# Four weight conversions of the second MLP, taken from the first two pairs of blocks into block 1

## The chip, the cores and the metric

The kernel runs on one core of a Trainium2 chip. The metric is the device time of one execution in microseconds; where several executions are timed, their median counts. TensorE is called PE in the profile, VectorE DVE, ScalarE ACT, GpSimd POOL and SyncE SP; POOL and SP issue nearly all of the transfers, each from a queue of its own.

## The reference

Attention in chunks of 64 over 8 x 8 heads of 576 x 64, then an MLP with softplus (512 to 2048 to 512), then a second one that takes the largest of three products (512 to 768) and multiplies it by w_out (768 to 512). There are 4608 tokens.

```python
scores = scale * np.matmul(q_c, k_c.transpose(0, 1, 2, 4, 3))      # chunks of 64
attn = np.exp(scores - max); attn = attn / (sum + 1e-09)
x = np.matmul(attn, v_c)                                           # 4608 x 512
h = x @ w_in
g = np.maximum(h, 0.0) + np.log1p(np.exp(-np.abs(h)))
x = g @ w_out                                                      # 4608 x 512
h = np.maximum(np.maximum(x @ w1, x @ w2), x @ w3)
out = h @ w_out2                                                   # 4608 x 512
```

The inputs come as float64, which the chip reads as pairs of 32-bit words. Each weight has to be turned into float32 by integer and float operations on DVE before it can be used.

## The kernel before

The tokens are nine blocks of 512. Blocks 0 to 2 go through the first MLP in steps (`mlp1`): step (b, j) is one h product of block b with the j-th of sixteen slices of w_in (L805, into `ph`), softplus on ACT, a cut into a high and a low part `g` on ACT and DVE (the L288 rows `g<-tmp,g`), and one o product (L825, into `acc`). Each product takes about 2.7 us of PE. The steps of the first two blocks are taken in turns: (0,0-3), (1,0-7), (0,4-15), (1,8-15), and then block 2. Blocks 3 to 8 go in three pairs; a pair's first product is made in eight units with seven products in place of eight (`UnitA`, L1120, into `ph` and `one`), its second one by `mlp1_out` (L1419, into `acc`), and in the last pair in another seven-product form (L1342). Beside this the attention of the later tokens runs in tiles: loads of q and k (L443) and v (L468), transposes on DVE (L698, L699), products into `aps` (L503), a softmax (ACT L562; DVE L554, L558, L590, L591), a transposed p (L751) that is stored to `pd` (L755) and read back turned (L760, `s<-pd`) by SP, and the next product. In the pairs the attention products go to `one` and the like (L597).

The units need differences of weight slices. `weightsa` makes them in blocks 1 and 2 on DVE and ACT from the slices that are still in SBUF, and POOL stores them to `wac` and `wae` (L1027); the units read them back on POOL's queue (L1045). The two halves of a pair also store parts to DRAM, such as `gd` and `wso` (L1233), and partial sums of the first two blocks go through `partd` (L782 reads them back into `tmp` buffers).

The second MLP comes last, and its weights are converted ahead of time by `early(n, due, after)`. There are 24 conversions: numbers 0 to 17 are slices of w1, w2 and w3, numbers 18 to 23 of the last w_out. A conversion of the first kind is
- a load of 512 KB from the input by POOL (L318, into an `s` slot),
- seven operations on DVE: L332, L339, L346, L351, L357, L360 and an add at L288 (`tmp<-tmp,tmp`), in two `tmp` buffers,
- a store of 256 KB to `w2d` by SP (L869).

All of it, with every other piece of work, is an operation of a planner. Each has a due time in an idealised clock (a step counts 5.44 us), the operations that it needs, and the buffers that it takes from pools. `Plan.order` then simulates the engines and starts, on each engine that comes free, the ready operation with the earliest due time; the order in which they start is the order of the program. Each engine, and each queue, then runs its own list in that order, so an instruction that waits holds up all that stands behind it on its engine. A conversion's load may not start before the product given in `after`; the last operation is due `EARLY` = 8 steps after the place from which it was asked. The table `EARLIES` says how many conversions each unit of each pair asks for. No more than two conversions are in the works at a time (a buffer called "early").

Of the kernel before, what the change touches and what calls it, by code (L numbers as in the profile page):

```python
# [183 lines left out]
def tile_kernel(ctx: ExitStack, tc: tile.TileContext, q, k, v, w_in, w_out, w1, w2, w3, wo2, out):  # L184
# [790 lines left out]
    EARLY = 8  # L975
    GATE = 7
    SPLITS = 6
    EARLIES = ((0, 0, 1, 1, 1, 1, 1, 1), (1,) * 8, (2, 2, 1, 1, 1, 1, 1, 1))
    GROUPS = (0, 1, 2, 3, 4, 6, 7)
    LATE_GROUPS = (1,)  # L980
    SPLIT = 1
# [716 lines left out]

    def strassen():

        outs, earlies = [], 0
        tile_at = HP * NP + 2 * HP + 2

        def out(n=1):
            last = None
            for out_of, *which in outs[:n]:
                last = out_of(*which)
            del outs[:n]
            return last

        def group():
            nonlocal tile_at
            if tile_at <= NTILE + 1:
                attention(tile_at, [first_loads[11]], True)
            tile_at += 1

        splita(0)
        pairs = (NB - NP) // 2
        for q in range(pairs):
            A, B = NP + 2 * q, NP + 2 * q + 1  # L1720
            old = None
            sevens = Sevens(q) if q in SEVENS else None

            def later(m, f):
                outs.append((sevens.along, m, f) if sevens else (mlp1_out, A, 2 * m + f))

            for n, m in enumerate(ORDER[q]):
                clock[0] = T0 + STEP * NJ * A + 17.7 * n
                new = UnitA(q, m)
                begin = new.p1()  # L1730
                mark["unit", q, n] = begin
                if ("unit", q, n) in COMBOS:
                    combos(COMBOS.index(("unit", q, n)), [begin], clock[0] + 30.0)
                if n == SEVENS_LOAD and sevens:
                    mark["sevens", q] = begin
                for _ in range(EARLIES[q][n]):
                    early(earlies, clock[0] + STEP * EARLY, [begin])
                    earlies += 1
                if q == pairs - 1:
                    mark[n] = begin  # L1740
                if not sevens:
                    out()
                if old:
                    old.p5()
                    old.p4()
                    if sevens:
                        out()
                    later(old.n, 1)
                new.p6()
                if old:  # L1750
                    old.p3()
                else:
                    out()
                new.p2()
                if not old:
                    out()
                new.p7()
                if n in GROUPS:
                    group()
                out()  # L1760
                later(m, 0)
                old = new
            clock[0] = T0 + STEP * NJ * A + 17.7 * (NJ // 2)
            mark["load", q] = begin
            mark["late", q] = old.p4()
            later(m, 1)
            out()
            old.p5()
            out()
            old.p3()  # L1770
            if sevens:
                outs.extend((sevens.step, p, n2) for p in (5, 4, 3, 6, 7) for n2 in range(NJ // 4))
                while len(outs) > (4 if q == pairs - 1 else 0):
                    out()
                continue
            todo = [(mlp1_out, B, 2 * m + f) for m in ORDER[q] for f in range(2)]
            outs.extend((*todo[i], (h,)) for h in range(2) for i in range(2))
            outs.extend(todo[2:])
            for j in range(NJ - 2):
                o = out()  # L1780
                if ("out", q, j) in COMBOS:
                    combos(COMBOS.index(("out", q, j)), [o], clock[0] + 30.0)
                if j in LATE_GROUPS:
                    group()
                if j == SPLIT and q + 1 < pairs:
                    splita(q + 1)
        mark[5] = mark[6]
        clock[0] = T1
        for late, at in enumerate((mark[FIRST], mark["step", *MORE[2]])):
            weights3(late, [at])  # L1790
        both = [Buf("ph"), Buf("ph"), Buf("aps", fresh=four_banks)]
        accs = [Buf("acc") for _ in range(2)]
        banks = [Bank(both[:1], lambda: both[2].t[0]), Bank(both[1:], lambda: both[2].t[1])]
        banks += [Bank([z], lambda z=z: z.t) for z in accs]
        D = range(NJ2 // 2)
        gate = [mark["step", *MORE[1]]]
        for q in range(NB // 3):
            u = Triple(q, banks, gate)
            u.g = {}
            todo = [(s, d) for d in D for s in (0, 1)] + [(s, d) for s in range(2, 12) for d in D]  # L1800
            todo += [(s, d) for d in D for s in (12, 13)] + [(14, d) for d in D]
            if q == 0:
                todo[:6] = [(0, 0), None, None, (1, 0), None, None, (0, 1), (2, 0), (0, 2), (1, 1), (1, 2)]
                todo = [p for n, p in enumerate(todo) if p != (2, 0) or n < 11]
            for p in todo:
                if p is None:
                    out()
                    continue
                begin = u.product(*p, alloc=both if both[0].first is None else [])
                if p == (11, 0):  # L1810
                    u.late = begin
                if p == (14, 2):
                    gate = [begin]
            for c in range(3):
                for d in D if (q, c) != (NB // 3 - 1, 2) else D[:-1]:
                    u.out(c, d)
            banks = [u.main[1], u.main[2], u.spare, u.main[0]]
        for h in range(2):
            u.out(2, D[-1], range(2 * h, 2 * h + 2))
# [17 lines left out]
    for j in range(NJ):  # L1837
# [4 lines left out]
        for t in range(HP, 2 * HP) if j == 1 else ():  # L1842
            attention_first(t, [line["load"]])
    tiles = 2 * HP
    for n, (b, j, first, last) in enumerate(steps):
        if n >= NJ and n % (NJ // HP) == 0:
            t = HP + n // (NJ // HP)
            t = 2 * HP + (n - NJ) // 2
            while tiles <= t + 1 and tiles < 22:
                attention(tiles, [first_loads[tiles if tiles < 2 * HP + 3 else NJ - 1]])  # L1850
                tiles += 1
        h = mlp1(b, j, first, last)
        if ("step", b, j) in COMBOS:
            combos(COMBOS.index(("step", b, j)), [h], T0 + STEP * (n + 4))
        if b == NP - 1 and j % 2 == 0:
            weightsa(j // 2, [before_last], lead)
        if (b, j) == (1, NJ // 2):
            lead = h
        before_last = h if j % 2 == 0 else before_last
# [38 lines left out]
```

## Time and profile before

| | us |
|---|---|
| median of three timed runs | 1371.14 |
| the three runs | 1365.4, 1371.14, 1371.9 |
| the profiled execution | 1365.48 |
| its span, first to last instruction | 1363.6 |
| busy: PE / DVE / ACT / POOL | 1333.2 / 983.7 / 545.0 / 321.7 |
| DMA moved | 289.38 MB, 212 GB/s in the mean |

The share of a busy engine is an average over stages. Blocks 0 to 2 fill the trace up to about 330 us, the pairs follow until about 840 us, and the second MLP is the rest. What a shift of work is worth is read from the stretch that it leaves and the stretch that it enters: which wait of PE ends there, what it waited for, and how long before their use the results of the other engines are ready. The granted PE clock is full in all of the stretches that are spoken of here (0.994 in the mean of the span, with the only drop near the start).

### The profile page before, as it was taken

What the parts mean: (1) busy time and instruction counts of PE and PEld (TensorE: products, weight loads), DVE (VectorE), ACT (ScalarE), POOL (GpSimd) and SP (SyncE); (2) the same over time, 40 slices, a digit from 0 to 9 for tenths busy, and PEclk for the clock granted to TensorE, in tenths of its full rate; (3) what the DMA queues carried; (4) which work ended last, traced back from release to release, by engine and by line L of the source; (5) the groups of instructions that cost most, each with busy time, mean ns of one, the idle gap of its engine ahead of it and who ended that gap; (6) DMA issues with size and microseconds to landing.
All of it is one profiled execution on the core that took longest, in us unless ns stands there. A gap on an engine that the chain in (4) does not pass through costs nothing.

```text
span 1363.6 us, 23089 instructions
## 1 busy us (share of the span) xinstructions
PE 1333.2 (98%) x8616; PEld 1094.0 (80%) x8616; DVE 983.7 (72%) x1527; ACT 545.0 (40%) x1199; POOL 321.7 (24%) x561
## 2 busy tenths in 40 slices
PE   5899999999999999999999999999999999999998
PEld 4788887888888887787788887888888888888887
DVE  8999965797576898657868898779714597145951
ACT  4544434464544645445535454432123222132211
POOL 2011555542233324323211122121111122011100
PEclk8999999999999999999999999999999999999999
DMA  8565567677689999978966789655644465344401
GB/s 254 159 201 154 134 181 201 189 273 228 169 257 258 267 302 301 280 252 297 366 209 237 259 311 338 234 192 193 219 162 144 155 231 206 141 148 154 139 25 68
DMA packets 218863, 289.38 MB, mean 212 GB/s; under 512 B 121601, under 2 KB 146625, under 8 KB 218753
## 3 DMA queue, kind: packets, MB, share of 16 engines
q0 software_dynamic: 53792, 178.26, 38.1%
q1 hardware_dynamic: 164144, 108.87, 26.9%
q8 instruction: 68, 1.11, 0.3%
q10 hardware_dynamic: 816, 0.79, 0.2%
q14 instruction: 43, 0.34, 0.1%
HBM read 196.61 MB, written 91.23 MB: 211 GB/s over the span
## 4 chain that ended last, share of the span: by engine, by line
PE 86%; DVE 5%; issue 4%; DMA 2%; POOL 1%; ACT 1%; SPq 0%; DVEq 0%; POOLq 0%; ACTq 0%
PE acc L1567 14%; PE both L1567 13%; PE acc L825 10%; PE ph L805 9%; PE ph L1120 8%; PE acc L1419 7%; PE one L1120 6%; PE both L1665 6%; PE acc L1665 5%; PE acc L1342 2%; PE ph L1342 2%; PE acc L1265 2%; DVE s L288 1%; PE aps L503 1%; POOL rv L468 1%
## 5 line engine op out<-in xcount | busy, mean ns | idle before, releaser
L288 DVE TENSOR_TENSOR s<-s,s 128x1024 f32<-128x1024 f32 (+3 forms) x222 | 213.8, 992 | 11.8 <-DMA x2d<-s 5.5
L1419 PE MATMUL acc<-g,s 128*128 128x512 f32 x768 | 184.5, 393 | 3.0 <-ACT tmp L281 2.2
L1419 PEld LDWEIGHTS acc<-g,s 128*128 128x128 f32 x768 | 142.6, 188 | 35.2 <-ACT tmp L281 3.1
L1120 PE MATMUL ph<-s,s 128*128 128x512 f32 x576 | 144.1, 389 | 1.4 <-DMA s<-wac 0.7
L805 PE MATMUL ph<-s,s 128*128 128x512 f32 x576 | 140.4, 394 | 0.0
L825 PE MATMUL acc<-g,s 128*128 128x512 f32 x576 | 139.8, 392 | 0.0
L1120 PEld LDWEIGHTS ph<-s,s 128*128 128x128 f32 x576 | 108.0, 188 | 24.6 <-DMA s<-wac 1.2
L805 PEld LDWEIGHTS ph<-s,s 128*128 128x128 f32 x576 | 108.3, 189 | 23.1
L825 PEld LDWEIGHTS acc<-g,s 128*128 128x128 f32 x576 | 107.3, 188 | 22.6
L281 ACT CAST s<-s 128x512 fp32r<-128x512 f32 (+1 forms) x106 | 86.3, 831 | 93.4 <-DVE s L1598 31.2
L1567 PE MATMUL acc<-s,s 128*128 128x512 f32 x452 | 120.3, 389 | 0.0
L1550 POOL DMA_DIRECT2D s<-w2c x105 | 56.0, 533 | 266.2 <-PE both L1567 87.5
L281 ACT CAST g<-s 128x1024 fp32r<-128x1024 f32 (+1 forms) x64 | 58.7, 919 | 144.6 <-PE both L1567 37.3
L1567 PE MATMUL acc<-g,s 128*128 128x512 f32 x400 | 110.0, 389 | 0.0
L1120 PE MATMUL one<-s,s 128*128 128x512 f32 x432 | 106.4, 390 | 0.9 <-ACT p L562 0.9
L1567 PE MATMUL both<-s,s 128*128 128x512 f32 x400 | 106.3, 389 | 0.0
L288 DVE TENSOR_TENSOR g<-tmp,g 128x512 fp32r<-128x512 f32 x104 | 70.6, 680 | 44.3 <-ACT g L281 44.2
L1567 PE MATMUL both<-g,s 128*128 128x512 f32 x368 | 100.1, 389 | 0.0
L1567 PEld LDWEIGHTS acc<-s,s 128*128 128x128 f32 x452 | 84.9, 188 | 17.6
L1120 PEld LDWEIGHTS one<-s,s 128*128 128x128 f32 x432 | 80.9, 188 | 18.5 <-ACT p L562 1.8
L468 POOL DMA_DIRECT2D rv<-in_v_dram x103 | 63.5, 620 | 104.5 <-issue 55.3
L1567 PEld LDWEIGHTS both<-s,s 128*128 128x128 f32 x400 | 75.1, 188 | 15.6
(158 smaller groups left out, 2159.5 us busy)
## 6 DMA issues: line engine op xcount, KB each, us to landing
s<-w2c POOLq DMA_DIRECT2D x105, 512.0 KB, 4.5
s<-wac POOLq DMA_DIRECT2D x66, 512.0 KB, 6.5
w2c<-s POOLq DMA_DIRECT2D x45, 512.0 KB, 5.2
wac<-s POOLq DMA_DIRECT2D x24, 512.0 KB, 5.1
s<-in_moe_w_dram POOLq DMA_DIRECT2D x18, 512.0 KB, 5.6
s<-x2d POOLq DMA_DIRECT2D x18, 512.0 KB, 5.8
s<-in_moe_w_in_dram SPq DMA_DIRECT2D x16, 512.0 KB, 6.2
s<-in_moe_w_out_dram SPq DMA_DIRECT2D x16, 512.0 KB, 5.7
```

What stands on the lines that cost most here:

```text
L281: nc.scalar.copy(dst(), src())
L288: return op({"D": 0.69 * n}, lambda e: nc.vector.tensor_tensor(dst(), a(), b(), f), r=r, w=w, **kw)
L468: dma(out=dst().rearrange("p (c e d) -> p c e d", e=2, d=D)[half * CH:(half + 1) * CH, lo:lo + mine, h, :], in_=v[b, t % HP * 2 + h].rearr ...
L805: nc.tensor.matmul(ph.t, w[:, wi, kk * P:(kk + 1) * P], x[kk].t[:, xi], start=(kk == 0 and wi == 0 and xi == 0), stop=(kk == KD - 1 and wi ...
L825: nc.tensor.matmul(acc[m // 2].t[:, m % 2], w[:, wi, m * P:(m + 1) * P], g.t[:, gi, :], start=(first and wi == 0 and gi == 0), stop=(last ...
L1120: nc.tensor.matmul(dst(), ws.t[:, wi, col + kk * P:col + (kk + 1) * P], x[kk].t[:, xi], start=(first and kk == 0 and wi == 0 and xi == 0), ...
L1265: nc.tensor.matmul(u.acc[f].t[:, m], w.t[:, wi, m * P:(m + 1) * P], g.t[:, gi, :], start=(first and wi == 0 and gi == 0), stop=(last and w ...
L1342: nc.tensor.matmul(dst(m), lhs(wi, nn, m), (GH, GL)[gi].t[:, nn], start=(fresh and nn == 0 and wi == 0 and gi == 0), stop=(nn == 1 and wi ...
L1419: nc.tensor.matmul(acc[half].t[:, m % 2], w.t[:, wi, m * P:(m + 1) * P], g.t[:, gi, :], start=(first and wi == 0 and gi == 0), stop=(last ...
L1550: lambda e, k=k, z=z: nc.gpsimd.dma_start(out=z.t.bitcast(F32), in_=w2c[s][late + k]),
L1567: nc.tensor.matmul(bank.view()[:, f], ws(wi, slice(f * HT + kk * P, f * HT + (kk + 1) * P)), (XH, XL)[xi].t[:, kk], start=(first and kk == ...
L1665: nc.tensor.matmul(banks[t // 2].view()[:, t % 2], (GH, GL)[gi].t[:, f, t * P:(t + 1) * P], wo2_of[j].t[:, wi], start=(j == 0 and wi == 0 ...
```

## The change

The table `EARLIES` loses four entries: units 6 and 7 of the first pair and units 0 and 1 of the second ask for no conversion any more. A new table `BEFORE` names four steps of block 1 (its slices 9, 11, 13 and 15), and each of these asks for one conversion behind its h product. The number of the next conversion is now an iterator that the steps and the units share, so the same 24 conversions are asked for in the same order: numbers 0 to 3 by block 1's second half, and every later one of the first pair from a place four conversions on. The due time is again eight steps after the place.

```diff
--- before.py
+++ after.py
@@ -975,7 +975,8 @@
     EARLY = 8
     GATE = 7
     SPLITS = 6
-    EARLIES = ((0, 0, 1, 1, 1, 1, 1, 1), (1,) * 8, (2, 2, 1, 1, 1, 1, 1, 1))
+    EARLIES = ((0, 0, 1, 1, 1, 1, 0, 0), (0, 0, 1, 1, 1, 1, 1, 1), (2, 2, 1, 1, 1, 1, 1, 1))
+    BEFORE = ((1, 9), (1, 11), (1, 13), (1, 15))
     GROUPS = (0, 1, 2, 3, 4, 6, 7)
     LATE_GROUPS = (1,)
     SPLIT = 1
@@ -1698,7 +1699,7 @@
 
     def strassen():
 
-        outs, earlies = [], 0
+        outs = []
         tile_at = HP * NP + 2 * HP + 2
 
         def out(n=1):
@@ -1734,8 +1735,7 @@
                 if n == SEVENS_LOAD and sevens:
                     mark["sevens", q] = begin
                 for _ in range(EARLIES[q][n]):
-                    early(earlies, clock[0] + STEP * EARLY, [begin])
-                    earlies += 1
+                    early(next(earlies), clock[0] + STEP * EARLY, [begin])
                 if q == pairs - 1:
                     mark[n] = begin
                 if not sevens:
@@ -1842,6 +1842,7 @@
         for t in range(HP, 2 * HP) if j == 1 else ():
             attention_first(t, [line["load"]])
     tiles = 2 * HP
+    earlies = iter(range(4 * NJ2 + 6))
     for n, (b, j, first, last) in enumerate(steps):
         if n >= NJ and n % (NJ // HP) == 0:
             t = HP + n // (NJ // HP)
@@ -1850,6 +1851,8 @@
                 attention(tiles, [first_loads[tiles if tiles < 2 * HP + 3 else NJ - 1]])
                 tiles += 1
         h = mlp1(b, j, first, last)
+        if (b, j) in BEFORE:
+            early(next(earlies), T0 + STEP * (n + EARLY), [h])
         if ("step", b, j) in COMBOS:
             combos(COMBOS.index(("step", b, j)), [h], T0 + STEP * (n + 4))
         if b == NP - 1 and j % 2 == 0:
```

Since the planner makes the order anew, other work moves too. On POOL's queue, at the end of the first pair's second product, one of the four places that are vacated (wso and wac are the stores and loads of the pairs, L318 is the conversion's load). Before:

```order
L1233 DMA wso_1_237<-s_252_5884 128x1024
L1233 DMA wso_1_241<-s_253_5898 128x1024
L318 DMA s_257_5933<-in_moe_w_dram 128x4x256
L1233 DMA wso_2_230<-s_258_5957 128x1024
L1233 DMA wso_2_234<-s_259_5974 128x1024
L1045 DMA s_262_6004<-wac_1_159 128x1024
L1233 DMA wso_2_238<-s_260_5985 128x1024
L1233 DMA wso_2_242<-s_261_5996 128x1024
```

Now (lines behind the table stand one further down):

```order
L1234 DMA wso_1_237<-s_254_5895 128x1024
L1234 DMA wso_1_241<-s_255_5910 128x1024
L1234 DMA wso_2_230<-s_259_5968 128x1024
L1234 DMA wso_2_234<-s_260_5989 128x1024
L1046 DMA s_263_6022<-wac_1_159 128x1024
L1234 DMA wso_2_238<-s_261_6001 128x1024
L1234 DMA wso_2_242<-s_262_6014 128x1024
```

The conversion's load is gone from between the wso stores, and the rest stands as it did. In the second half of block 1, on DVE, behind an attention tile's mx (p and mx belong to the softmax, s<-rq and s<-tmp are the transposes of q and k, g is the cut that the next o product reads). Before:

```order
L558 TENSOR_SCALAR mx_71<-mx_71 128x8
L288 TENSOR_TENSOR s_113_2790<-aps_94,s_113_2790 128x512
L698 STREAM_TRANSPOSE s_114_2811<-rq_74 128x512
L699 STREAM_TRANSPOSE s_114_2811<-tmp_78 128x512
L590 TENSOR_SCALAR mx_70<-mx_70 128x8
L591 RECIPROCAL mx_70<-mx_70 128x8
L288 TENSOR_TENSOR p_89<-p_89,mx_70 128x512
L751 STREAM_TRANSPOSE s_115_2853<-p_89 128x512
```

Now:

```order
L558 TENSOR_SCALAR mx_71<-mx_71 128x8
L332 TENSOR_SCALAR tmp_86<-s_110_2638 128x512
L698 STREAM_TRANSPOSE s_114_2811<-rq_74 128x512
L339 TENSOR_SCALAR tmp_86<-tmp_86 128x512
L699 STREAM_TRANSPOSE s_114_2811<-tmp_78 128x512
L346 TENSOR_SCALAR tmp_86<-tmp_86 128x512
L351 SCALAR_TENSOR_TENSOR tmp_86<-s_110_2638,tmp_86 128x512
L590 TENSOR_SCALAR mx_70<-mx_70 128x8
L357 TENSOR_SCALAR tmp_79<-tmp_86 128x512
L591 RECIPROCAL mx_70<-mx_70 128x8
L360 SCALAR_TENSOR_TENSOR tmp_79<-s_110_2638,tmp_79 128x512
L288 TENSOR_TENSOR p_89<-p_89,mx_70 128x512
```

The first conversion's operations stand between the transposes and the softmax, and the difference of the scores (`s<-aps,s`) comes later. On SP, in the same half block (pd is the stored softmax, partd the partial sums). Before:

```order
L755 DMA pd_90<-s_118_3009 128x512
L443 DMA tmp_84<-in_q_dram 32x8x32
L468 DMA rv_88<-in_v_dram 64x3x64
L468 DMA rv_88<-in_v_dram 64x64
L468 DMA rv_88<-in_v_dram 64x4x64
L782 DMA tmp_79<-partd_98 128x512
L782 DMA tmp_86<-partd_98 128x512
L760 DMA s_118_3009<-pd_90 32x2x256 x4
```

Now:

```order
L869 DMA w2d_105<-tmp_78 128x2x256
L443 DMA tmp_85<-in_q_dram 32x8x32 x4
L755 DMA pd_90<-s_121_3027 128x512
L782 DMA tmp_84<-partd_98 128x512
L443 DMA tmp_85<-in_q_dram 32x8x32 x2
L468 DMA rv_88<-in_v_dram 64x3x64
L468 DMA rv_88<-in_v_dram 64x64
L782 DMA tmp_81<-partd_98 128x512
L782 DMA tmp_80<-partd_98 128x512
L782 DMA tmp_78<-partd_98 128x512
L443 DMA tmp_85<-in_q_dram 32x8x32
L760 DMA s_121_3027<-pd_90 32x2x256 x4
```

A store to w2d from tmp_78 has come in, a load of partd goes into that same buffer, and the four loads of pd stand behind it. On PE the same products stand in the same order, but for the attention product that reads these loads: it stood ahead of one o product, and stands behind it now.

## Rows read from the trace of the kernel before

**Rows 1.** The page, part 1: engine, busy us, share of the span, instructions.
```profile
PE 1333.2 (98%) x8616; PEld 1094.0 (80%) x8616; DVE 983.7 (72%) x1527; ACT 545.0 (40%) x1199; POOL 321.7 (24%) x561
```

**Rows 2.** Waits of PE, 440 to 560 us: us in total, times, longest.
```profile
PE one L1120 <- ACT p L562: 0.9, 2, 0.6
PE ph L1120 <- DMA s<-wac: 0.7, 1, 0.7
PE acc L1419 <- DVE g L288: 0.4, 1, 0.4
PE acc L1419 <- ACT tmp L281: 0.3, 1, 0.3
```

**Rows 3.** Windows: length, busy us (instructions) by engine, granted clock, DMA share, GB/s.
```profile
220.00:240.00 20.00, 18.89 (x199) 15.27 (x199) 12.82 (x28) 9.28 (x41) 10.55 (x18) 1.00 0.67 159
...
540.00:560.00 20.00, 18.65 (x139) 14.62 (x138) 11.47 (x23) 8.79 (x28) 8.97 (x15) 1.00 1.00 287
```

**Rows 4.** Timeline of DVE, first operations of conversions: start, us, operation, [idle before].
```profile
434.43 0.52 DVE L332 TENSOR_SCALAR tmp<-s 128x512 int32<-128x512 int32 x1
...
511.38 0.42 DVE L332 TENSOR_SCALAR tmp<-s 128x512 int32<-128x512 int32 x1
...
531.54 0.43 DVE L332 TENSOR_SCALAR tmp<-s 128x512 int32<-128x512 int32 x1 [0.72 <-DMA s<-in_moe_w_dram]
...
550.56 0.43 DVE L332 TENSOR_SCALAR tmp<-s 128x512 int32<-128x512 int32 x1 [3.85 <-DMA s<-in_moe_w_dram]
```

**Rows 5.** The chain of waits, 540 to 560 us: start, us, what.
```profile
544.62 5.92 DMA s<-in_moe_w_dram
...
557.14 1.65 PE one L1120 x6
```

**Rows 6.** Groups of DVE by form, 344 to 600 us: count, busy us, mean ns.
```profile
L351 DVE SCALAR_TENSOR_TENSOR tmp<-s,tmp 128x512 int32<-128x512 int32 x12 | 8.2, 686 | 0.3
...
L332 DVE TENSOR_SCALAR tmp<-s 128x512 int32<-128x512 int32 x12 | 5.3, 445 | 6.5 <-DMA s<-in_moe_w_dram 6.5
```

**Rows 7.** Timeline of SP, 540 to 560 us.
```profile
545.60 0.44 SPq L869 DMA_DIRECT2D w2d<-tmp  x1
```

**Rows 8.** Windows of blocks 1 and 2, columns as in rows 3.
```profile
211.90:337.50 125.60, 124.49 (x1015) 101.84 (x1014) 95.68 (x198) 61.87 (x214) 57.64 (x99) 1.00 0.71 212
...
260.00:320.00 60.00, 60.00 (x498) 49.09 (x498) 56.57 (x118) 33.89 (x110) 24.55 (x43) 1.00 0.65 213
```

**Rows 9.** Timelines of DVE and PE: a g, and its o product.
```profile
215.03 0.65 DVE L288 TENSOR_TENSOR g<-tmp,g 128x512 fp32r<-128x512 f32 x1
...
226.02 2.88 PE L825 MATMUL acc<-g,s 128*128 128x512 f32 x12
```

**Rows 10.** Timelines of DVE and PE where the first pair begins.
```profile
330.44 0.68 DVE L288 TENSOR_TENSOR g<-tmp,g 128x512 fp32r<-128x512 f32 x1
...
337.53 0.69 DVE L288 TENSOR_TENSOR tmp<-one,tmp 128x512 f32<-128x512 f32 x1 [4.59 <-PE one L1120]
...
338.71 0.69 PE L597 MATMUL one<-s,tmp 64*64 64x64 f32 x32
```

**Rows 11.** Waits of PE, 200 to 240 us.
```profile
PE aps L503 <- DMA s<-pd: 1.1, 2, 0.6
```

**Rows 12.** Timelines of SP and PE, the third attention product of this stretch.
```profile
235.93 1.78 SPq L760 DMA_DIRECT2D s<-pd  x4
...
243.75 0.69 PE L503 MATMUL aps<-s,tmp 64*64 64x64 f32 x32
```

**Rows 13.** DMA issues: queue, count, KB each, median us to landing.
```profile
s<-pd SPq DMA_DIRECT2D x112, 64.0 KB, 4.0
...
w2d<-tmp SPq DMA_DIRECT2D x18, 256.0 KB, 4.7
```

**Rows 14.** Two lines by themselves: ns min/median/max, first and last start, form.
```profile
L318 POOL DMA_DIRECT2D s<-in_moe_w_dram x18: 753/775/799, 366.4 to 700.2; - x18
...
L332 DVE TENSOR_SCALAR tmp<-s x22: 411/420/528, 374.0 to 754.1; 128x512 int32<-128x512 int32 x22
```

## The prediction

> **What bounds the kernel now.** I read the shares of the engines first. TensorE is busy 1333.2 us, 98% of the span of 1363.6 [rows 1], so all that any re-ordering can win is its 30.4 us of idle time, and most of that lies at the start, which this edit leaves alone. I then asked, stretch by stretch, what TensorE waits for where the four conversions are taken away. Between 440 and 560 us there are five waits of 2.3 us in all [rows 2]. That is the whole prize. The last 20 us of it hold 1.35 us (18.65 busy of 20), with the DMA engines fully busy [rows 3].
>
> Next I looked at which wait belongs to which conversion. The places that are vacated are units 6 and 7 of the first pair and units 0 and 1 of the second; their first operations (L332) run between 434.4 and 531.5, the third of the four at 511.4. The conversion that begins at 550.56 belongs to the second pair's unit 2. It stays, and it is the one that DVE stops 3.85 us for [rows 4]. The chain of waits goes through exactly that load (5.92 us from 544.62), through the softmax behind it, into the product at 557.14 [rows 5]. So the waits fall in two parts: 1.0 us (0.4 of g, 0.3 of tmp, 0.3 of p) stands behind vacated conversions, at 461, 519 and 522; 1.35 us (0.7 of the wac load, 0.6 of p) stands behind one that is not moved at all.
>
> **The change, part by part.** A conversion is one 512 KB load on POOL's queue, seven DVE operations and one 256 KB store on SP's. DVE: four operations like L332 at 0.45 us, two like L351 at 0.69, and an add of the same width, put at 0.69 too [rows 6], together 1.8 + 2.1 = 3.9 us; four conversions make 15.4 us. Nothing is added or removed over the whole kernel; TensorE's list is the same but for one attention product that now stands behind an o product of 2.7 us and not ahead of it. All 15.4 us change place, beside four loads and four stores.
>
> *What the old place gets back.* By the order of the rows, DVE has some 4 us less to do just ahead of the wait at 461, and some 3 us less ahead of the two near 520. I count these three as gone: -1.0 us. The two at 552 and 557 I count half. For them speaks that the vacated conversion's last store is issued at 545.60, between the two loads that matter [rows 7], into engines that are full; 256 KB of 287 GB/s [rows 3] is 0.9 us. Against it: the load at 544.62 and its place in the queue are unchanged, and its landing would have to come down by the 0.6 us that TensorE waits. Bounds 0 and -1.35; I take -0.7.
>
> *What the new place pays on DVE.* From 211.9 to 337.5 us DVE is busy 95.68 of 125.60 [rows 8], so 29.9 us are free, twice the 15.4. What matters is whether results keep their lead. A g that DVE ends at 215.7 is read at 226.0, 10.3 us later [rows 9]; from the order at most 7.9 us of DVE work stands newly ahead of any product between 221 and 250, and part of that is work done in idle time. So the g's are covered. If that cover were gone, each us beyond it would be a us of TensorE. The weight differences (two reads of s, then half-width operations and casts) that stood here are pushed back behind the conversions. Most of them fall on idle time too; but a last piece now stands directly before `tmp<-one,tmp` of 337.53, of which TensorE's transposes at 338.71 have 0.5 us to spare [rows 10]. Before, DVE sat idle 4.59 us there; now about 7.0 us of work stands between the last g (at 330.44) and it, which gives 330.44 + 0.65 + 7.0 = 338.1, a tie with 338.0 plus whatever DVE is late when it arrives. Between 260 and 320 it was 56.57 of 60 busy [rows 8], so lateness from block 1 is not worked off quickly. Bounds 0 and 2; I take +0.7.
>
> *What it pays on the queues.* The products at 221.2 and 222.1 already wait 1.1 us for s<-pd [rows 11], so any later landing there is paid in full. In the order POOL now issues the first 512 KB load ahead of five wac stores, close before that; the stretch's DMA share is 0.67 [rows 3], so some of it fits. Bounds 0 and 1.8 (512 KB at the 287 GB/s of [rows 3], nothing hidden); I take +0.4. On SP the four stores cost 0.4 us of issue time each. More important is what stands behind them: a load of partd into a tmp buffer now follows a w2d store out of that buffer, so SP waits for the store to land, and the four s<-pd loads of the next attention product are queued behind this wait. Before, these were issued at 235.93 for the product at 243.75, which they met with about 2 us to spare [rows 12]; the product has moved 2.7 us back, so some 4.5 us are there. The conversion ends near 230; a store lands in 4.7 us at the median, a s<-pd load in 4.0 [rows 13]: 230 + 4.7 + 2 of issues + 4.0 = 240.7, in time against 246.5; with the longest store landing of 9.0 us and 7 us for the loads 248, 1.5 late. I take +0.4.
>
> *The sum*: -1.0 - 0.7 + 0.7 + 0.4 + 0.4 = -0.2 us, bounds -2.4 and, with nothing won in the old place, +5.3. On the profiled execution (1365.48, the span and 1.9 us around it) that is 1365.3. The three timed runs are 1365.4, 1371.14 and 1371.9; their median is the measure, so the forecast is 1371.0, and a median of other runs can lie up to 6 us lower with no change of the kernel.
>
> **A rule weighed.** What the rows show: L318 takes POOL 753 to 799 ns in all 18 of its issues, and L332 takes DVE 411 to 528 ns in all 22 that the trace holds [rows 14], though the two engines work at once in most of the stretch; neither ever took a whole operation of the other longer. The Trainium skill (SBUF — State Buffer, "Who interferes with whom") says that some VectorE modes and GpSimd share a port pair which one holds for its whole instruction while the other stands still, and its section "SBUF: two separate sides" warns that descriptors of GpSimd's DMAs can starve for it. By that rule the move is against us: the conversions go from a stretch where POOL is little used to one where it prepares 57.64 of 125.60 us [rows 8]. The trace so far shows 0.1 us of scatter at most, so I put nothing in the sum for it.
>
> **The rivals.**
> *SP's queue turns late (slower).* Place: the w2d store, the partd load and the s<-pd loads queued on SP in block 1's second half, with the loads of 222, 231 and 246. For it: the first of them is already late, and each s<-pd group is issued behind more. Against: leads of 4 to 5 us on the other two. If landings go from 4.0 to the 9.0 us that a store has needed, +5.0 at 222, about +0.5 at each of the other two, with +0.7 at 338 and -1.0 to -1.7 of the old place: about +5, 1376. It decides once a s<-pd group lands over 5 us later than before at a product with lead, or over 2 at 222. Chance 0.16.
> *The lock (slower).* Each of sixteen short operations waits out a POOL preparation of about 0.6 us: 9.6 us more for DVE, 25 in all against 29.9 free, which cannot all be used; what is left over falls on 338: about +4, 1375. Chance 0.04.
> *The whole prize and more (faster).* A less crowded DVE and DMA take all 2.4 us, and also the 2.0 us wait at 645 and 0.7 at 690 behind them: -5, 1366. Against: from 543 us on the order of DVE is the same up to a constant 2 us, so nothing moves near 645. Chance 0.10.
> *Nothing gained in the old place.* The three waits are handed on to ACT or to loads that were just in time, and the new costs are covered too: 1371.1. Chance 0.08.
>
> **How the numbers follow.** The forecast, a change within -2.4 and +2.5, has 0.62: 1371.0. The range takes in the slower rival's 1376 and, below, a median out of the lower half of the run times shown with a small gain: 1364 to 1376.5. About 0.5% (6.9 us) is what a measurement can tell here from no change. Faster by more needs the larger gain, or the forecast's gain met by a low median: 0.16. Slower by more needs the queue rival at its upper end: 0.11. Within: 0.73.
>
> **What would show it.** Right: in the changed kernel's trace no wait of TensorE at 461 and 519 to 522, waits of 0 to 1.35 us near 552 and 557 with the load still 4 to 6 us long, 1 to 2 us at 222, at most 2 us near 338, and TensorE's busy sum unchanged. Wrong: waits for s<-pd of 2 us or more at 231 or 246 (the queue), L332 over 0.8 us in block 1 (the lock), a wait for DVE at g between 221 and 330 (cover misjudged), or the waits after 600 us changed by more than 1 us, for which my reading has no reason.

## The result, and the profile after

The changed kernel is slower: its median is 1381.12 us (six runs, 1378.01 to 1386.86) against 1369.61 for the kernel before (six runs, 1365.4 to 1371.9), a ratio of 1.0093 with a 95% interval of 1.0072 to 1.0113. The forecast was 1371.0 and its range ended at 1376.5, so the time lies outside it, on the side of the rival that was given 0.16.

The profiled execution of the changed kernel took 1384.83 us with a span of 1382.8. It is one of the longer ones of this kernel, and the one of before (1365.48) one of the shorter, so the 19 us between the two profiles are more than the 11.5 us between the medians. What the profiles show well is where it is lost. TensorE has the same products in the same order but for one, so the start of the n-th product can be laid beside the start of the same product before:

| product that began before at | what is there | later by, in all | step |
|---|---|---|---|
| 54 | start-up | -1.0 | |
| 223 | after the two attention products that waited 1.1 us | -2.5 | -1.4 |
| 233 to 236 | block 1, attention product | 5.5 | +8.0 |
| 245 to 250 | block 1, next attention product (moved behind an o product) | 10.6 | +5.1 |
| 290 | block 1, o product | 16.0 | +5.4 |
| 340 | first pair begins | 17.7 | +1.7 |
| 559 | old place of the conversions ends | 14.8 | -2.9 |
| 574 | one softmax later | 15.9 | +1.1 |
| 649 | second pair, second product | 18.3 | +2.4 |
| last | | 18.9 | +0.6 |

So 18.5 us are lost within 70 us of block 1 and what follows it, and the old place gives back two to three. Three waits do it. PE's waits from 195 to 345 us of the changed kernel (us in total, times, longest; compare [rows 11]):

```profile
PE aps L503 <- ACT p L562: 6.0, 1, 6.0
PE acc L825 <- DVE g L288: 3.5, 1, 3.5
PE aps L503 <- DMA s<-pd: 3.3, 1, 3.3
```

The three waits are 12.8 us, and 18.5 are lost. The rest is the clock. In the windows (columns as in [rows 3]) the granted clock falls below 1.00 just where PE has waited:

```profile
220.00:240.00 20.00, 13.95 (x164) 11.46 (x154) 6.89 (x15) 5.88 (x22) 10.91 (x19) 0.83 0.52 139
240.00:260.00 20.00, 16.74 (x126) 13.55 (x125) 13.54 (x26) 6.32 (x28) 8.74 (x15) 0.91 0.71 190
300.00:320.00 20.00, 19.77 (x196) 15.90 (x197) 19.77 (x43) 11.94 (x34) 5.37 (x10) 0.91 0.70 249
```

Before, PE was busy 18.89 of the 20 us from 220 and the clock was full [rows 3]. PE's busy sum rises too, from 1333.2 [rows 1] to 1337.5, with the same products:

```profile
PE 1337.5 (97%) x8616; PEld 1096.7 (79%) x8616; DVE 984.5 (71%) x1529; ACT 547.0 (40%) x1197; POOL 319.4 (23%) x558
```

Why PE waited is read on DVE. Its timeline in block 1 and behind it (start, us, operation, in brackets the idle time before it and what ended it); L332 begins a conversion, L554 begins a softmax, L751 ends one:

```profile
208.31 0.43 DVE L332 TENSOR_SCALAR tmp<-s 128x512 int32<-128x512 int32 x1 [0.93 <-DMA s<-in_moe_w_dram]
...
230.72 0.43 DVE L332 TENSOR_SCALAR tmp<-s 128x512 int32<-128x512 int32 x1 [11.73 <-DMA s<-in_moe_w_dram]
...
231.52 0.68 DVE L554 TENSOR_REDUCE mx<-aps 128x8 f32<-128x512 f32 x1
...
243.51 0.43 DVE L332 TENSOR_SCALAR tmp<-s 128x512 int32<-128x512 int32 x1 [5.77 <-DMA s<-in_moe_w_dram]
243.85 0.70 DVE L751 STREAM_TRANSPOSE s<-p 128x512 f32<-128x512 f32 x1
...
297.28 0.71 DVE L698 STREAM_TRANSPOSE s<-tmp 128x512 f32<-128x512 f32 x1 [9.44 <-DMA wac<-s]
```

The first conversion's load was in time but for 0.9 us. The second stopped DVE for 11.73 us, the third for 5.77 (and the fourth, not shown, for 4.54). DVE takes its list in order, so the L554 of an attention tile at 231.52 and the L751 at 243.85 stood behind them, and behind these ACT's exponentials, the store and the read of pd, and PE:

```profile
232.69 0.31 ACT L562 ACTIVATE p<-aps,mx 128x64 f32<-128x64 f32 x1 [11.25 <-DVE mx L558]
...
235.22 1.18 PE L503 MATMUL aps<-s,rv 64*64 64x64 f32 x30 [6.05 <-ACT p L562]
...
255.34 0.86 PE L503 MATMUL aps<-s,tmp 64*64 64x64 f32 x29 [3.26 <-DMA s<-pd]
256.91 4.32 PE L805 MATMUL ph<-s,s 128*128 128x512 f32 x12
...
300.23 4.37 PE L825 MATMUL acc<-g,s 128*128 128x512 f32 x11 [3.47 <-DVE g L288]
```

ACT idled 11.25 us for mx and PE 6.05 for ACT; the next attention product came 3.26 us late through pd; the twelve h products behind it took 4.32 us where 2.88 is usual. The third wait of PE, for the g at 300.23, has no conversion in front of it: that g stood behind the L698 of 297.28, a transpose of q, and this for 9.44 us behind a store to wac. And why the loads were late is read on POOL (L318 is the conversion's load, L443 the k loads, L1028 the stores to wac):

```profile
202.48 0.77 POOL L318 DMA_DIRECT2D s<-in_moe_w_dram  x1 [3.32 <-issue]
203.25 1.62 POOL L1028 DMA_DIRECT2D wac<-s  x3
208.60 1.18 POOL L1028 DMA_DIRECT2D wac<-s  x2 [3.73 <-issue]
...
226.03 0.78 POOL L318 DMA_DIRECT2D s<-in_moe_w_dram  x1 [0.85 <-issue]
227.00 0.61 POOL L443 DMA_DIRECT2D tmp<-in_k_dram  x1 [0.20 <-issue]
231.00 1.90 POOL L443 DMA_DIRECT2D tmp<-in_k_dram  x3 [3.39 <-issue]
...
237.19 0.79 POOL L318 DMA_DIRECT2D s<-in_moe_w_dram  x1
239.21 1.16 POOL L468 DMA_DIRECT2D tmp<-in_v_dram  x2 [1.23 <-issue]
243.82 0.64 POOL L468 DMA_DIRECT2D tmp<-in_v_dram  x1 [3.45 <-issue]
...
287.95 3.01 POOL L443 DMA_DIRECT2D tmp<-in_k_dram  x5 [0.46 <-issue]
290.94 1.14 POOL L1028 DMA_DIRECT2D wac<-s  x2
```

"issue" means that POOL waited for nothing that the profile shows. Behind each L318 (the fourth, at 259.37, is not shown) it handed over one to three more transfers and then stood for 3.4 to 3.7 us. DVE's L332 at 230.72 shows when the load of 226.03 had landed, and POOL went on at 231.00; the load of 237.19 was there for the L332 of 243.51, and POOL went on at 243.82. So POOL's queue moved again just as the large load had landed. DVE executed nothing through all but the last 0.3 us of POOL's stand at these two places (it idled from 219 to 230.72 and from 237.7 to 243.51), so an operation of DVE that holds POOL up is not the reason. The second load itself came out only at 226.03, 23.5 us after the first: it stood in the same queue behind k loads that leave one by one. On SP's queue, at the same place of the program (E3 below), it went out 18.3 us after the first, at 217.55. The store to wac that the L698 of 297.28 waited for left the same queue, behind five k loads.

### The profile page after: what moved, and what is told of

Read it like the earlier page. It is cut to its first block, busy times and chain, and to the rows that moved or that the text cites. A ratio compares the mean times of both kernels' runs of the same rounds, so it can differ in the third digit from the quotient of the medians.

```text
span 1382.8 us, 23107 instructions
## 1 busy us (share of the span) xinstructions
PE 1337.5 (97%) x8616; PEld 1096.7 (79%) x8616; DVE 984.5 (71%) x1529; ACT 547.0 (40%) x1197; POOL 319.4 (23%) x558
## 4 chain that ended last, share of the span: by engine, by line
PE 72%; DVE 11%; issue 6%; DMA 5%; POOL 3%; ACT 1%; SPq 1%; DVEq 0%; POOLq 0%; ACTq 0%
PE acc L1568 14%; PE both L1568 12%; PE acc L1420 7%; PE ph L1121 7%; PE acc L825 7%; PE ph L805 6%; PE both L1666 6%; PE one L1121 6%; PE acc L1666 5%; DVE s L288 5%; POOL tmp L443 1%; DVE tmp L288 1%; PE acc L1266 1%; DVE g L288 1%; POOL rv L468 1%
## 5 line engine op out<-in xcount | busy, mean ns | idle before, releaser
L1420 PEld LDWEIGHTS acc<-g,s 128*128 128x128 f32 x768 | 143.9, 189 | 34.6 <-ACT tmp L281 2.8
L825 PEld LDWEIGHTS acc<-g,s 128*128 128x128 f32 x576 | 109.1, 191 | 27.3 <-DVE g L288 3.9
L281 ACT CAST s<-s 128x1024 fp32r<-128x1024 f32 (+1 forms) x101 | 84.0, 844 | 89.8 <-DVE s L288 33.3
L288 DVE TENSOR_TENSOR tmp<-one,tmp 128x512 f32<-128x512 f32 x72 | 49.6, 689 | 54.0 <-PE one L1121 53.5
L1568 PEld LDWEIGHTS acc<-g,s 128*128 128x128 f32 x400 | 75.1, 188 | 15.6
```

The costliest lines, as they stand in the source:

```text
L281: nc.scalar.copy(dst(), src())
L288: return op({"D": 0.69 * n}, lambda e: nc.vector.tensor_tensor(dst(), a(), b(), f), r=r, w=w, **kw)
L825: nc.tensor.matmul(acc[m // 2].t[:, m % 2], w[:, wi, m * P:(m + 1) * P], g.t[:, gi, :], start=(first and wi == 0 and gi == 0), stop=(last ...
L1420: nc.tensor.matmul(acc[half].t[:, m % 2], w.t[:, wi, m * P:(m + 1) * P], g.t[:, gi, :], start=(first and wi == 0 and gi == 0), stop=(last ...
L1568: nc.tensor.matmul(bank.view()[:, f], ws(wi, slice(f * HT + kk * P, f * HT + (kk + 1) * P)), (XH, XL)[xi].t[:, kk], start=(first and kk == ...
```

## The experiments

All runs of an experiment are compared with runs of the kernel before on the same chip. "Same order" means that every engine has the changed kernel's instructions in the changed kernel's order.

**E1, without the loads.** The four conversions of block 1 read a weight slice that is already in SBUF.

```diff
 def load(e):
+    if how == "none":          # numbers 0 to 3
+        return
...
+at = lambda: wbuf["a", 15, 0].t.bitcast(I32).rearrange("p w (c t) -> p (w c) t", t=2) if how == "none" else raw.t
-hw = lambda: raw.t[:, :, 1]
+hw = lambda: at()[:, :, 1]
```

> The changed kernel with the four 512 KB loads in block 1 left out: the four conversions there read a weight slice that has long been in SBUF, so w2d gets wrong values; every other instruction of every engine is the same, in the same order. Theory A (the second, third and fourth conversions' first operation stands on DVE 18.4 us in all for loads that POOL issues late, and the softmax behind it is late for TensorE): no wait at L332 in block 1, the waits of 6.0, 3.3 and 3.5 us at the attention products and the o product go, time 1368 to 1372 against 1381. Rival B (15 us of DVE work are too much for the stretch): the waits shrink little, 1378 or more. Rival C (SP's queue: the w2d stores and the partd loads behind them): a wait for s<-pd of 3 us stays, about 1376.

Measured: 1366.21 us, ratio 0.9976 (0.9957 to 0.9994). Of PE's waits between 195 and 345 us only this one is left:

```profile
PE one L602 <- DVE tmp L288: 1.1, 1, 1.1
```

All 15 us of DVE work and the four stores are still there. They cost nothing in block 1, and rivals B and C fall. What is left is the 1.1 us where the first pair begins, which the prediction had at 0.7.

**E2, without DVE's part.** The loads stay, the seven operations of these four conversions go, and their stores send a resident slice.

```diff
-lambda e: nc.vector.tensor_scalar(ai(), hw(), 0x7FFFFFFF, None, ALU.bitwise_and),
+unless(off, lambda e: nc.vector.tensor_scalar(ai(), hw(), 0x7FFFFFFF, None, ALU.bitwise_and)),   # and the other six
```

> The counterpart: the four loads in block 1 stay where they are, but the seven DVE operations of each of these four conversions are left out, and their stores send a resident weight slice, so w2d gets wrong values. Theory A: nothing on DVE waits for the loads, so TensorE's waits between 225 and 305 us go although the loads land as late as before: 1367 to 1371. Rival B gives the same. Rival D (the loads themselves crowd the DMA engines or POOL's queue, and k, v and pd arrive late): 1376 or more, with waits for s<-pd or at L699.

Measured: 1378.69 us, ratio 1.0069 (1.0043 to 1.0095). This was against theory A. No DVE instruction waits for a conversion's load any more, and most of the loss stays. DVE's and PE's waits:

```profile
DVE s L702 <- DMA tmp<-in_k_dram: 17.4, 3, 7.6
...
DVE s L701 <- DMA wac<-s: 8.2, 1, 8.2
...
PE acc L828 <- DVE g L288: 4.6, 1, 4.6
PE aps L506 <- DMA s<-pd: 3.8, 1, 3.8
```

DVE now waits 17.4 us for k loads at the k transpose (L702 in this kernel). L332 was only what stood first in line: behind it DVE would have waited for k loads from the same queue. The longest wait of PE, 4.6 us for g, stands behind another instruction, the transpose of q (L701 here), which waited 8.2 us for a store to wac, also from POOL's queue. Theory A had the wait right and the cause too far down; rival D was right that the loads themselves crowd POOL's queue. What was still to be told apart was bytes, pieces and queue.

**E3, the loads on SP's queue.** Same order, same bytes.

```diff
-start = (nc.gpsimd if e == "G" else nc.sync).dma_start
+start = (nc.gpsimd if e == "G" and how != "sp" else nc.sync).dma_start
```

> The changed kernel, same order on every engine, with the four block 1 loads issued by SP's queue at the same place of the program and not by POOL's. Theory A with POOL's backlog as the cause of the late loads: the landing of the second to fourth load comes earlier by some us, the waits at L332 fall from 18.4 us to under 6, time 1370 to 1375. If the loads are late for another reason (their place in the order is late on any queue, or a slot comes free late): L332 waits as long as now, 1379 to 1383.

Measured: 1370.96 us, ratio 1.0022 (1.0008 to 1.0035). PE's largest wait there, and what DVE waits for at the conversions:

```profile
PE aps L505 <- DMA s<-pd: 2.5, 1, 2.5
...
DVE tmp L334 <- DMA s<-in_moe_w_dram: 1.4, 1, 1.4
```

18.4 us at L332 became 1.4. The same 2 MB in the same stretch cost 0.2% and not 0.9%. So it is not the bandwidth; it is POOL's queue. SP's queue has its own price, the 2.5 us for s<-pd.

**E4, one conversion moved.** `BEFORE = ((1, 9),)`, and only unit 7 of the first pair vacated; the planner orders anew.

> Only one conversion is moved: step (1, 9) asks for it, and only unit 7 of the first pair asks for none; the planner makes its order anew. The first of the four had its load in time (DVE waited 0.9 us). Theory A: no wait of over 2 us at L332 in block 1, time within 3 us of the kernel before (1367 to 1372). Rival B or C, in proportion: a quarter of the 11.5 us, 1372.5.

Measured: 1371.27 us, ratio 1.0026 (1.0007 to 1.0044). In block 1 nothing is lost: PE's only wait between 195 and 345 us is 0.5 us. But this kernel's profile, its longest run of ten, loses 5 us at 534, 3 more by 555 and nearly 5 between 640 and 668, most of it in waits that the changed kernel has not got at those places or, the first, not as long (2.4 us):

```profile
PE acc L1420 <- ACT tmp L281: 4.0, 1, 4.0
PE one L597 <- DVE tmp L288: 3.1, 1, 3.1
PE ph L1121 <- DMA s<-wac: 2.2, 1, 2.2
```

So a single load in block 1 is free, and the loss is not in proportion. What a new order does to the pairs, 200 us later, is as large as what the change was about; why this order loses there was not looked into, and the run settles nothing more.

**E5, fewer pieces.** The four loads bring 512 KB as 128 runs of 4 KB, on POOL's queue, same order. As they were, a load is 512 runs of 1 KB; a k load of 32x8x32 is 256 runs.

```diff
+if how == "wide":
+    start(out=raw.t.rearrange("p f t -> p (f t)"), in_=src[:P, :8 * P])
```

> The changed kernel, same order everywhere, the four block 1 loads still on POOL's queue and still 512 KB, but read in 128 runs of 4 KB from the input and not in 512 runs of 1 KB, so the weights that they bring are wrong. DVE waits for them as before. Theory P (POOL's queue takes only so many pieces at a time; behind a load of 512 pieces POOL can hand over almost nothing until it has landed, and the k loads behind it are late): POOL stands much shorter behind these loads, L332 and L699 wait under 5 us in all, time 1368 to 1373. Theory Q (the bytes of these loads, or any large load among the k loads): 1377 to 1383 as with the change.

**E6, fewer bytes.** 512 pieces of 256 bytes; the conversions read a resident slice as in E1.

```diff
+start(out=raw.t.rearrange("p (k f) t -> p k (f t)", k=KD)[:, :, :P // 2],
+      in_=src[:, j * 2 * P:j * 2 * P + P // 2].rearrange("(k p) f -> p k f", p=P))
```

> The converse: the four block 1 loads keep their 512 pieces but bring 256 bytes each, 128 KB and not 512 KB; DVE's conversions there read a resident weight slice and wait for nothing, so w2d gets wrong values. Against the run without these loads, only the four small loads on POOL's queue are added. Theory P: POOL stands behind them for as long as they take to land, the k loads are late, L699 waits: 1374 to 1380. Theory Q: a quarter of the bytes, 1367 to 1370.

E5 measured 1370.90 us, ratio 1.0028 (1.0011 to 1.0044). DVE waits and PE waits:

```profile
DVE tmp L336 <- DMA s<-in_moe_w_dram: 11.4, 2, 7.3
...
PE aps L507 <- DMA s<-pd: 3.6, 4, 1.5
```

The time is in theory P's range, its waits are not: DVE still stood 11.4 us for two of these loads, where under 5 had been expected. Yet only 0.3% was lost. Behind these loads POOL stood 1.9 to 3.2 us and not 3.4 to 3.7, and DVE waited for no k load, though POOL's unexplained idle time before all k loads from 200 to 300 us is hardly less in sum (25.6 us, 26.0 with the change). E6 measured 1370.71 us, ratio 1.0025 (1.0009 to 1.0041):

```profile
DVE s L707 <- DMA wac<-s: 8.3, 1, 8.3
DVE s L708 <- DMA tmp<-in_k_dram: 7.1, 2, 5.0
...
PE acc L834 <- DVE g L288: 4.2, 1, 4.2
```

Small loads with as many pieces still hold up the k loads, 7.1 us at the k transpose, but far less than E2's 17.4, and PE does not wait there. Its 4.2 us are for a g behind the transpose of q (L707), which stood 8.3 us for the store to wac; in E1, without the loads, the same transpose stood 3.8 us and PE did not wait. Theory P expected 1374 to 1380 and was too simple. That a load's pieces are in the way for as long as the load takes to land, so that both count, would fit the two runs, but was not tested further. Neither alone gives the 0.9%.

**E7 and E8, more descriptor memory.** The kernel is built with 1024 bytes a partition for the descriptors of POOL's transfers. Here it is 1536, for the changed kernel (E7) and the kernel before (E8). The identity matrix shares the buffer p to make room.

```diff
-ident = pool.tile([P, P], F32, name="ident")
+p_tile = mem("p", 1, [P, TB], F32)
+ident = p_tile[0][:, :P]
...
-"p": mem("p", 1, [P, TB], F32),
+"p": p_tile,
...
-dynamic_dma_scratch_size=1024
+dynamic_dma_scratch_size=1536
```

> The changed kernel with the memory that POOL's queue has for its descriptors raised from 1024 to 1536 bytes a partition (the identity matrix moves into the buffer p to make room; same order). Theory P: POOL's idle time between k loads and behind the 512 KB loads shrinks, the waits in block 1 fall by at least half: 1368 to 1375. If the limit is not that memory: 1378 to 1383.

> The kernel before with the same 1536 bytes: POOL's idle time between the k loads of blocks 1 and 2 shrinks if the memory is the limit, and the 1.1 us wait for s<-pd near 222 is not its doing. Time 1363 to 1369; equal to before within 0.3% if nothing of the path hangs on POOL there.

E7 measured 1366.25 us, ratio 0.9982 (0.9966 to 0.9998); E8 1362.39 us, ratio 0.9955 (0.9939 to 0.9971). The group of POOL's k loads from 200 to 300 us (count, busy us, mean ns, idle us before them and what ended it), in the kernel before, in E8, in the changed kernel, and in E7:

```profile
L443 POOL DMA_DIRECT2D tmp<-in_k_dram x49 | 28.9, 592 | 30.6 <-issue 29.1 <-DVE s L698 0.8 <-DMA rv<-in_v_dram 0.3
```

```profile
L444 POOL DMA_DIRECT2D tmp<-in_k_dram x48 | 28.1, 591 | 15.6 <-issue 6.8 <-DMA x2d<-tmp 3.5 <-DVE g L289 1.6
```

```profile
L443 POOL DMA_DIRECT2D tmp<-in_k_dram x48 | 28.4, 596 | 31.7 <-issue 26.0 <-DMA rv<-in_v_dram 3.2 <-DMA tmp<-in_q_dram 1.5
```

```profile
L444 POOL DMA_DIRECT2D tmp<-in_k_dram x48 | 28.7, 603 | 22.1 <-issue 16.3 <-DMA x2d<-tmp 1.9 <-DMA rq<-in_q_dram 1.5
```

A k load takes POOL as long as ever (0.59 us). What falls is the time in which POOL stood still before one without a reason in the profile: 29.1 to 6.8 us in the kernel before, 26.0 to 16.3 in the changed one. With half as much memory again, the changed kernel gets back all that it lost, though not all of it in block 1: in E7's profile PE still waits 3.0 us there behind the first operation of a conversion, and has lost 4 us more by 320 us than in E8's. With the same memory, the kernel before is still 3.9 us ahead of it. The Trainium skill (DMA: Bandwidth & Descriptors, "SWDGE vs HWDGE vs iDMA") says that GpSimd writes the descriptors of its transfers into rings in SBUF, from which the engines drain them. These runs agree so far as that memory is what they change: with more of it, POOL waits less.

**E9, the control.** The identity in p, 1024 bytes, kernel before.

> The kernel before with the identity matrix in the buffer p, and the descriptor memory left at 1024 bytes: the control for the two runs with 1536. If the memory made those faster: equal to before within 0.2% (1365 to 1370) and POOL's idle time that nothing in the profile explains, 33 us between 200 and 300 us, is still there. If the place of the identity did it: 1362.

Measured: 1369.44 us, ratio 1.0003 (0.9986 to 1.0020). The identity's place does nothing to the time. The k loads of this profile:

```profile
L444 POOL DMA_DIRECT2D tmp<-in_k_dram x48 | 28.2, 589 | 28.8 <-issue 20.3 <-DMA tmp<-in_q_dram 4.6 <-DVE mx L592 1.2
```

So with 1024 bytes the unexplained idle time is 20.3 us here and 29.1 above: single profiles differ by some 9 us. The 6.8 of E8 (7.3 in E12, the same kernel once more) lies clear of that; the fall in the changed kernel, from 26.0 to 16.3, does not by itself, and there the time is the better witness.

**E10 and E11, 1728 bytes**, for the changed kernel and the kernel before.

> The changed kernel with 1728 bytes, the dose above 1536. If POOL's queue is what the change runs into, the one wait that was left in block 1 (3.0 us behind a conversion's load) shrinks further: 1361 to 1365. If it stays at 1366, what is left is the change's place itself.

> The kernel before with 1728 bytes. With 1536, POOL's unexplained idle time between 200 and 300 us fell from 33 to 7 us, so little is left to win: 1360 to 1363. Against the changed kernel with the same memory this also shows what the change is worth when its loads are in time: by its old place alone -2 us, by 338 and 640 to 650 us about +2.

E10 measured 1369.74 us, ratio 1.0011 (0.9997 to 1.0025); E11 1368.52 us, ratio 1.0000 (0.9986 to 1.0014). Both expectations missed. POOL's unexplained idle time before k loads is as short as with 1536 bytes (7.2 us in E11, 14.9 in E10), so the queue is relieved; but in E10 loads still stop DVE, for 4.9 us in all, where it was 3.0 us with 1536 bytes:

```profile
DVE tmp L333 <- DMA s<-in_moe_w_dram: 4.9, 2, 4.4
```

and in E11 the profile loses 4 us between 486 and 539 and gets 3.4 back by 645. Why the larger memory gives the kernel before nothing, with as little idle time of POOL, is open. For the changed kernel both sizes win back most or all of the loss (1.0011 and 0.9982 against 1.0093).

**E12, E8 once more**, with five rounds.

> The kernel before with 1536 bytes once more, since 1728 bytes gave no gain over the kernel before though POOL's unexplained idle time was as short. If the 0.45% is a gain of the memory: 0.993 to 0.998 again. If it was the chip or the order of the runs: 0.998 to 1.002.

Measured: 1362.85 us, ratio 0.9959 (0.9942 to 0.9976). The gain is there again, some 5.6 us. So the kernel before with 1536 bytes is the fastest version found, faster than both kernels. Where its gain lies, and that it comes from POOL's shorter idle time, is not shown: in E8's profile the wait at 645 is gone (-2.0 us) and 2.0 us are gained around the two near 555; E12's profiled execution, one of its longer ones, shows less, and E11 had as little idle time and no gain.

## Why the prediction was wrong, point by point

**The sign and the place.** The forecast had no change; the slower rival had SP's queue, 1376. The slower side was right and the mechanism was not. Of its three places the one at 222 got better: the 1.1 us wait [rows 11] is gone. The one at 246 did lose 3.3 us for s<-pd, as the rival had it, but not by the w2d store and the partd load: the pd store itself stood behind DVE's 5.77 us at L332. E1 has the same stores and partd loads and no such wait.

**The step that failed** is "what the new place pays on DVE". It compared 15.4 us of work with 29.9 us of free time [rows 8] and the lead of the results, and took each conversion's work as ready when its turn came. It never asked when the load behind L332 would land, though [rows 4] showed an L332 that had stopped DVE for 3.85 us in the old place. The work was free, as E1 shows (0.9976 with all of it); the wait was not. Two of its own signs of being wrong came true: a wait for s<-pd of over 2 us near 246 (3.3), and one for g between 221 and 330 (3.5), though the g was late behind a wait of DVE and not behind work.

**The term that was mis-sized** is the load in "what it pays on the queues": +0.4 us, by its bytes, bounds 0 and 1.8. E1 against the changed kernel puts the four loads at about 16 us (0.9976 to 1.0093 of 1369); E3 beside E1 (1.0022 and 0.9976) leaves under 0.5% for their bytes and for SP's queue together. A row that would have warned was in the trace of before and was not used: the first of the groups shown with E7 and E8, k loads with 30.6 us of idle time before them, 29.1 of it "issue". The prediction named POOL's 57.64 us busy of 125.60 [rows 8] only for the lock, and did not ask what the other 68 were. Some 37 of them were "issue", time in which POOL stood for nothing that the profile shows, before the four loads came on top.

**The old place** comes out near its forecast in sum, -1.7 us forecast and -1.8 found at 574 (from 17.7 to 15.9 in the table), but not by its parts, so the sum is luck. Of the three waits behind vacated conversions the two at 461 and 519 are gone; the third, for a softmax at 522, is still there and has grown from 0.3 to 1.0 us (at 539.4 now), against the prediction's sign that it would go. Both waits behind the conversion that stays, counted half, are gone, and a new one of 0.5 us stands one softmax later. In the runs with the same order the same stretch gives back 1.4 (E10) to 3.5 us (E1, E5, E6). In the second pair a wait that was taken to stay is longer, the second of these two:

```profile
PE one L1121 <- ACT p L562: 1.0, 1, 1.0
...
PE acc L1420 <- ACT tmp L281: 2.4, 1, 2.4
```

**The first pair's begin**: +0.7 forecast; PE waits 1.1 us there. It does so in E1 too, so the loads are not needed for it; but in E7 and E10, the same order with more descriptor memory, the wait is gone, so the order alone does not make it either.

**No reason near 645**: the prediction said that a change of over 1 us there would be against its reading. It was +2.4 us in the profile. The wait at 645, 2.0 us before and 2.4 with the change, is 3.6 in E1, without the loads, and 0 to 0.7 in the five profiles with more descriptor memory. So it seems to hang on POOL's queue as well; by which transfer was not tried, and E5, with 1024 bytes, has no wait there either.

**The lock** did not show. L332 takes DVE as long in block 1 as elsewhere, beside POOL's transfers:

```profile
L332 DVE TENSOR_SCALAR tmp<-s x19: 418/420/519, 208.3 to 738.6; 128x512 int32<-128x512 int32 x19
```

**TensorE's busy sum** was said to stay. It rose by 4.3 us, which fits the lower clock after the waits.

Three readings were wrong and bear on nothing here: a step of the planner's clock counts 6 us, not 5.44; the trace of before holds 56 L332 and not 22, which are those from 374 us on (all 56 take 361 to 528 ns); and the 0.7 us wait put at 690 lies at 681.

## What to carry to other kernels

Work that is moved into an engine's free time takes its inputs along: for each moved instruction that waits for a transfer, ask which queue issues the transfer there, what stands ahead of it, and who stands behind the waiting instruction. An engine that issues transfers is not half free because it is half busy: here its idle time with no releaser in the profile, before transfers of many short runs, was mostly a queue that was full, since more memory for its descriptors took most of it away, and the large loads put into it were late and made others late. If a few hundred bytes of that memory can be found, try it before any re-ordering, and try more than one size: here 1536 bytes were worth 0.4%, more than the 2.3 us of waits that there were to win in the old place [rows 2], and 1728 bytes nothing.

## What the runs showed of the hardware

- POOL stood still after handing over a load of 512 runs of 1 KB until the load had landed (3.4 to 3.7 us behind each of the four), and in the kernel before POOL stood up to 3.5 us before a k load (256 short runs for one of 32x8x32) without a reason in the profile. From 1024 to 1536 bytes of descriptor memory a partition, this unexplained idle time before the k loads from 200 to 300 us fell from 29.1 (20.3 in E9) to 6.8 us (7.3 in E12).
- After PE had waited 6.05, 3.26 and 3.47 us in block 1, its granted clock was 0.83, 0.91 and 0.91 in the 20 us windows, that is, the lower of its two levels (1.2 against 2.4 GHz) for part of them. Twelve products took 3.95 to 4.37 us (eleven of them in the last case) and not 2.88. The three waits of 12.8 us so became 18.5 us of delay. The 2.0 us wait at 645 of the kernel before came with no such drop; where the changed kernel waited 2.4 us there, the next window has 0.91.
- The landing time of a conversion's load hardly differs (median 5.6 us before, 5.1 after). Those of the four in block 1 took 4.7 to 6.3 us. What differs is when a load is issued.
